# The 64-row chunk of a down projection on the two halves of the TensorE array, two token tiles at a time

## The chip, the cores and the metric

The kernel runs on one core of a Trainium2 chip. The metric is the device time of one execution in microseconds (us). A fast run has a granted TensorE clock (the clock that the chip lets the engine have) of 0.999 or 1.0 of full speed.

The profiles name the engines PE (TensorE, matmuls), PEld (TensorE loading weights), DVE (VectorE), ACT (ScalarE), POOL (GpSimd) and SP (SyncE, which issues most DMAs). PSUM is where matmuls add up their results; the kernel uses it in banks of 512 columns. In the down projection a matmul loads a tile's hidden values into the array as weights and streams columns of `w_down` past them; the 128 or 64 rows are the F columns that it sums over.

## The reference

An attention branch and a GEGLU feed-forward branch work on the same x (2048 tokens of width D = 640) and are mixed by a gate of each token. The change touches the last line of the feed-forward branch.

```python
g = sigmoid((x * gate_w).sum(-1, keepdims=True))
a = A_ref(x, wqkv, w_phi, wo)                     # linear attention with a softmax feature map, then @ wo
b = (gelu(x @ w_gate) * (x @ w_up)) @ w_down      # F = 1728 hidden columns
out = g * a + (1 - g) * b
```

F = 1728 is 13 chunks of 128 and one chunk of 64. Inputs and output are bf16.

## The kernel before

Each of the 16 token tiles (128 tokens) accumulates one result in PSUM: 14 chunks of F (hidden values times `w_down`) and then 5 chunks of the attention output times `wo`. Four tiles make a block. A block first computes its hidden values (gate and up products, stage `gateup`) and then runs `down` four times. The attention output of a tile (`num`) is computed in between; it uses PSUM banks 2 to 5 and about ten VectorE operations.

The last chunk of F has 64 real rows. The kernel before pads it with zeros to 128 rows and multiplies it like any other:

```python
# loads(): rows 0-63 of chunk 13 are zero, rows 64-127 real
sc.op("pool", lambda e: e.memset(self.wd_sb[0:64, 13, :], 0.0), writes=["wdz"])
sc.dma("sp", lambda e: e.dma_start(self.wd_sb[64:128, 13, :], self.wd[13 * P:self.F, :]), writes=["wd13"])
# ... (cut)
# gateup(), chunk 13: gate in rows 0-63 and up in rows 64-127 of one bank; the product goes to rows 64-127
sc.op("dve", lambda e: e.tensor_tensor(
    self.hT[64:128, c, :], self.ps[64:128, bk * 512:bk * 512 + 512], self.gl[64:128, slot, :], ALU.mult), ...)
# ... (cut)
def down(self, t, banks):                       # one token tile
    halves = ((banks[0], 0, 320), (banks[1], 320, 320))     # the last tile: 512 and 128 columns
    def step(c, bk, w0, w):
        if c < self.NFC:                        # NFC = 14 chunks of F, the last one half zeros
            sc.op("pe", lambda e: e.matmul(self.bank(bk, w), self.hT[:, c, tt * P:(tt + 1) * P],
                                           self.wd_sb[:, c, w0:w0 + w], start=(c == 0), stop=False), ...)
        else:                                   # 5 chunks of the attention output
            k = c - self.NFC
            sc.op("pe", lambda e: e.matmul(self.bank(bk, w), self.goT[:, gs, k, :],
                                           self.wo_sb[:, k, w0:w0 + w], start=False, stop=(k == self.KD - 1)), ...)
    # ... (cut) all steps, then ScalarE reads the two banks out and a DMA stores the tile
def ffn(self):
    pairs = [(6, 7), (0, 1)]                    # PSUM banks, in turn
    for b in range(self.NB):
        at = {2: 4 * b + 1, 6: 4 * b + 2, 10: 4 * b + 3}    # num(t) after these chunks; block 0 has its own list
        # ... (cut) gateup of 14 chunks, with num() as `at` says
        for t in range(4):
            self.down(4 * b + t, pairs[self.pn % 2])
            self.pn += 1
            if b == 0 and t == 0:
                self.num(3)
            if b < self.NB - 1 and t == 2:
                self.num(4 * b + 4)             # the next block's first tile
```

The softmax here doesn't subtract the row's maximum and nothing guards it: scores larger than these inputs give would overflow.

Of the kernel before, what the change touches and what calls it, by code (L numbers as in the profile page):

```python
# [3 lines left out]
P = 128  # L4
# [3 lines left out]
ALU = mybir.AluOpType  # L8
# [95 lines left out]
class _Kernel:  # L104
# [6 lines left out]
    NFC = 14  # L111
# [92 lines left out]
    def loads(self):  # L204
        sc, nc = self.sc, self.nc
# [22 lines left out]
        def xblock(b):  # L228
            sc.dma("sp", lambda e: e.dma_start_transpose(
                self.xT[:, :, b * self.BT:(b + 1) * self.BT], self.x[b * self.BT:(b + 1) * self.BT, :]),  # L230
                writes=[("xT", t) for t in range(b * 4, b * 4 + 4)])
# [2 lines left out]
        wload(self.wqT, 0, "wqT")  # L234
        xblock(2)
        xblock(3)
        sc.op("pool", lambda e: e.memset(self.wd_sb[0:64, 13, :], 0.0), writes=["wdz"])
        half = 7 * P
        g3 = self.wg.rearrange("(kt p) n -> p kt n", p=P)
        u3 = self.wu.rearrange("(kt p) n -> p kt n", p=P)  # L240
        for i, (a, b) in enumerate(((0, half), (half, 13 * P))):
            sc.dma("sp", lambda e, a=a, b=b: e.dma_start(self.wg_sb[:, :, a:b], g3[:, :, a:b]), writes=[("wg", i)])
            sc.dma("sp", lambda e, a=a, b=b: e.dma_start(self.wu_sb[:, :, a:b], u3[:, :, a:b]), writes=[("wu", i)])
            if i == 0:
# [1 line left out]
                sc.dma("sp", lambda e: e.dma_start(self.wgu_sb[:, :, 64:128], u3[:, :, 13 * P:self.F]), writes=["wgu1"])  # L246
        sc.dma("sp", lambda e: e.dma_start(self.wd_sb[:, 0:13, :],
                                           self.wd[0:13 * P, :].rearrange("(c p) n -> p c n", p=P)), writes=["wd"])
        sc.dma("sp", lambda e: e.dma_start(self.wd_sb[64:128, 13, :], self.wd[13 * P:self.F, :]), writes=["wd13"])
        sc.dma("sp", lambda e: e.dma_start(self.wo_sb[:, :, :], self.wo.rearrange("(kt p) n -> p kt n", p=P)),  # L250
               writes=["wo"])

# [7 lines left out]
        for i in range(KD):  # L260
            n = self.HHI[i] - self.HLO[i] + 1
# [9 lines left out]
        for i in range(KD):  # L271
            n = self.HHI[i] - self.HLO[i] + 1
# [332 lines left out]
    def gateup(self, b, c, banks):  # L605
        sc = self.sc
        xs = lambda kt: self.xT[:, kt, b * self.BT:(b + 1) * self.BT]
        xr = [("xT", t) for t in range(4 * b, 4 * b + 4)]
        oldw = self.oldw
        slot = self.gn % 3  # L610
        self.gn += 1
        if c < 13:
            i = 0 if c < 7 else 1
            for w, wk, bk in ((self.wg_sb, "wg", banks[0]), (self.wu_sb, "wu", banks[1])):
                for kt in range(self.KD):
                    sc.op("pe", lambda e, kt=kt, w=w, bk=bk: e.matmul(  # L616
                        self.bank(bk), w[:, kt, c * P:(c + 1) * P], xs(kt), start=(kt == 0), stop=(kt == self.KD - 1)),
                        reads=xr + [(wk, i)], writes=[("ps", bk)], signal=(kt == self.KD - 1))
            sc.op("act", lambda e: e.activation(self.gl[:, slot, :], self.bank(banks[0]), AF.Gelu_apprx_tanh),  # L619
                  reads=[("ps", banks[0])], writes=[("gl", slot)], guard=oldw)  # L620
            sc.op("dve", lambda e: e.tensor_tensor(self.hT[:, c, :], self.bank(banks[1]), self.gl[:, slot, :], ALU.mult),  # L621
                  reads=[("ps", banks[1]), ("gl", slot)], writes=[("hT", c)], guard=oldw)
        else:
            bk = banks[0]
            for kt in range(self.KD):
                sc.op("pe", lambda e, kt=kt: e.matmul(  # L626
                    self.bank(bk), self.wgu_sb[:, kt, :], xs(kt), start=(kt == 0), stop=(kt == self.KD - 1)),
                    reads=xr + ["wgu0", "wgu1"], writes=[("ps", bk)], signal=(kt == self.KD - 1))
            sc.op("act", lambda e: e.activation(self.gl[64:128, slot, :], self.ps[0:64, bk * 512:bk * 512 + 512],
                                                AF.Gelu_apprx_tanh),  # L630
                  reads=[("ps", bk)], writes=[("gl", slot)], guard=oldw)
            sc.op("dve", lambda e: e.tensor_tensor(
                self.hT[64:128, c, :], self.ps[64:128, bk * 512:bk * 512 + 512], self.gl[64:128, slot, :], ALU.mult),
                reads=[("ps", bk), ("gl", slot)], writes=[("hT", c)], guard=oldw)

    def num(self, t):
        sc = self.sc
# [43 lines left out]
        sc.dma("sp", lambda e: e.dma_start_transpose(self.goT[:, gs, :, :], self.Og[:, sl, :]),  # L681
               reads=[("Og", sl)], writes=[("goT", gs)], guard=old)

    def down(self, t, banks):
        sc = self.sc
        tt = t % 4
        gs = t % 6
        os_ = t % 3
        last = t == self.NT - 1
        halves = ((banks[0], 0, 512), (banks[1], 512, 128)) if last else ((banks[0], 0, 320), (banks[1], 320, 320))  # L690

        def step(c, bk, w0, w):
            if c < self.NFC:
                sc.op("pe", lambda e: e.matmul(  # L694
                    self.bank(bk, w), self.hT[:, c, tt * P:(tt + 1) * P], self.wd_sb[:, c, w0:w0 + w],
                    start=(c == 0), stop=False),
                    reads=[("hT", c)] + (["wd13", "wdz", "hTz"] if c == 13 else ["wd"]), writes=[("ps", bk)], signal=False)
            else:
                k = c - self.NFC
                sc.op("pe", lambda e: e.matmul(  # L700
                    self.bank(bk, w), self.goT[:, gs, k, :], self.wo_sb[:, k, w0:w0 + w],
                    start=False, stop=(k == self.KD - 1)),
                    reads=[("goT", gs), "wo"], writes=[("ps", bk)], signal=(k == self.KD - 1))

        def evac(bks, w0, n):
            src = self.pair(bks) if len(bks) == 2 else self.bank(bks[0], n)
            dst = self.outsb[:, os_, w0:w0 + n]
            if len(bks) == 2:
                dst = dst.rearrange("p (b c) -> p b c", c=320)
            sc.op("act", lambda e: e.activation(dst, src, AF.Copy, scale=self.Gm[:, t:t + 1]),  # L710
                  reads=[("ps", k) for k in bks] + ["Gm"], writes=[("outsb", os_, w)for w in ((0, 320) if n == 640 else (w0,))])
            rows = self.out[t * P:(t + 1) * P, :]
            if t < self.TB:
                rows = self.out[0:self.BT, :].rearrange("(p j) n -> p j n", j=self.TB)[:, t, :]
            sc.dma("sp", lambda e: e.dma_start(rows[:, w0:w0 + n], self.outsb[:, os_, w0:w0 + n]),
                   reads=[("outsb", os_, w) for w in ((0, 320) if n == 640 else (w0,))], writes=[("out", t, w0)])
        n = self.NFC + self.KD
        if last:
            for bk, w0, w in halves:
                for c in range(n):  # L720
                    step(c, bk, w0, w)
                evac((bk,), w0, w)
        else:
            for c in range(n):
                for bk, w0, w in halves:
                    step(c, bk, w0, w)
            evac(banks, 0, 640)

    NUMB = 2
    oldw = [(w, k) for w in ("wv", "wk2", "wq2") for k in range(5)] + ["wgate"]  # L730

    def ffn(self):
        self.gn = 0
        self.pn = 0
        self.sc.op("pool", lambda e: e.memset(self.hT[0:64, 13, :], 0.0), writes=["hTz"], guard=self.oldw)
        pairs = [(6, 7), (0, 1)]
        for b in range(self.NB):
            if b == 0:
                order = [0, 1, 13] + list(range(2, 13))
                at = {8: 0, 11: 1, 13: 2}  # L740
            else:
                order = list(range(14))
                at = {2: 4 * b + 1, 6: 4 * b + 2, 10: 4 * b + 3}
            for idx, c in enumerate(order):
                if b == 0 and c == 13:
                    self.gateup(b, c, (2,))
                else:
                    self.gateup(b, c, pairs[self.pn % 2])
                    self.pn += 1
                if b == 0:  # L750
                    if idx == 0:
                        self.gram(14)
                    if idx == 3:
                        self.gram(15)
                        self.kv_evac()
                        self.gates()
                    if idx == 6:
                        self.kv_mask()
                if idx in at:
                    self.num(at[idx])  # L760
            for t in range(4):
                self.down(4 * b + t, pairs[self.pn % 2])
                self.pn += 1
                if b == 0 and t == 0:
                    self.num(3)
                if b < self.NB - 1 and t == 2:
                    self.num(4 * b + 4)
def bass_gated_mix__linear_kernel_hedgehog__geglu_ffn__prompt_kernel(
    nc: bass.Bass,
    A_x: bass.AP,  # L770
    A_wqkv: bass.AP,
    A_w_phi: bass.AP,
    A_wo: bass.AP,
    B_x: bass.AP,
    B_w_gate: bass.AP,
    B_w_up: bass.AP,
    B_w_down: bass.AP,
    gate_w: bass.AP,
    out: bass.AP,
):  # L780
    _Kernel(nc, A_x, A_wqkv, A_w_phi, A_wo, B_x, B_w_gate, B_w_up, B_w_down, gate_w, out).run()
# [28 lines left out]
```

## Time and profile before

| | before |
|---|---|
| device time, median of 3 runs | 299.86 us (299.65 to 300.2) |
| span of the profiled run | 297.8 us |
| TensorE (PE) busy | 292.9 us, 98% |
| feed-forward stage in the chain (first gate matmul to the last matmul) | 84.72 to 295.08 us: 210.36 us |

The first lines are from the page of the kernel before: the share of busy time, the chain that ended last, and the largest group of the down projection (L694 is the matmul of the 14 chunks of F; L700, in the chain below, that of the 5 attention chunks).

```profile
span 297.8 us, 4821 instructions
PE 292.9 (98%) x1913; PEld 171.9 (58%) x1913; DVE 162.2 (54%) x318; ACT 104.3 (35%) x183; POOL 29.0 (10%) x58
PE 96%; DMA 1%; ACT 1%; issue 0%; SPq 0%; ACTq 0%
...
L694 PE MATMUL ps<-wd_sb,hT 128*128 128x320 bf16 (+2 forms) x448 | 63.6, 299 | 0.0
```

PE is the bottleneck, and in the feed-forward stage the chain never leaves it. The 299 ns of one matmul is not its cost, since matmuls overlap. The chain in order of time gives the cost; its columns are the start in us, the length in us, and what it was. These are the start of the feed-forward stage, block 1's change from gate/up (L616, L626) to its down projection, the `num` insert for the next block (L649), and the end:

```profile
84.72 1.24 PE ps L616 x5
...
168.25 1.08 PE ps L626 x5
169.33 3.80 PE ps L694 x28
173.14 1.36 PE ps L700 x10
...
184.82 0.69 PE ps L649 x12
185.51 3.80 PE ps L694 x28
189.31 1.36 PE ps L700 x10
190.67 6.47 PE ps L616 x30
...
294.79 0.29 PE ps L700 x5
```

A tile takes 28 matmuls in 3.80 us, 0.136 us each, and then 10 more at the same pace. Two of the 28 belong to the half-empty chunk. Over 16 tiles that chunk costs 30 x 0.136 us and, for the last tile, 0.216 + 0.056 us: 4.35 us, half of it spent on zeros.

A table of windows tells where VectorE works: here a gate/up stage and the down projection after it (the columns are the window, then busy time with the count of instructions for PE, weight loads, DVE, ACT, POOL, then clock, DMA share and GB/s).

```profile
138.13:169.33 31.20, 31.20 (x173) 15.29 (x172) 18.83 (x43) 8.56 (x14) 4.29 (x4) 1.00 0.10 22
169.33:190.67 21.34, 21.34 (x166) 15.54 (x164) 4.07 (x11) 2.97 (x4) 1.27 (x1) 1.00 0.15 32
```

DVE has 12 us free in the first and 17 us free in the second.

### The profile page before, as it was taken

Reading aid. Unit: us, or ns where it says so; the run is one execution under the profiler, and the core shown is the slowest. Engines: PE = TensorE matmul, PEld = TensorE weight load, DVE = VectorE, ACT = ScalarE, POOL = GpSimd, SP = SyncE. Lnnn points to the kernel's source line nnn. Section 1 sums busy time; section 2 is a strip of 40 time slices with the busy share of each in tenths; the row PEclk is TensorE's granted clock in tenths of the full one; section 3 lists DMA queues with packets and bytes.
Section 4 is the critical chain, followed back from the end, with each engine's and each line's share of the span. In section 5 each row is a group of like instructions: output and inputs, shape, how many; then the busy total and the mean of one; then the engine's idle time right before and its main releaser. Section 6 shows DMA issues by size and latency. Waiting matters only on the chain.

```text
span 297.8 us, 4821 instructions
## 1 busy us (share of the span) xinstructions
PE 292.9 (98%) x1913; PEld 171.9 (58%) x1913; DVE 162.2 (54%) x318; ACT 104.3 (35%) x183; POOL 29.0 (10%) x58
## 2 busy tenths in 40 slices
PE   7999999999999999999999999999999999999996
PEld 3576656555544556775555577655457765545763
DVE  1348999998875679514655700455580045567000
ACT  3367787576663221121222212122221212232111
POOL 7000000000000011201011100101110010111000
PEclk9999999999999999999999999999999999999999
DMA  7999990000002122112011200201101010110101
GB/s 219 211 209 335 355 350 18 0 0 2 0 2 53 35 20 28 47 44 66 3 22 22 20 27 24 60 6 25 22 9 37 22 46 23 22 24 0 44 24 44
DMA packets 38098, 18.77 MB, mean 63 GB/s; under 512 B 30203, under 2 KB 37820, under 8 KB 38076
## 3 DMA queue, kind: packets, MB, share of 16 engines
q1 hardware_dynamic: 37424, 18.44, 24.4%
q8 instruction: 15, 0.25, 0.3%
q10 hardware_dynamic: 652, 0.03, 0.1%
q14 instruction: 7, 0.06, 0.1%
HBM read 8.96 MB, written 2.62 MB: 39 GB/s over the span
## 4 chain that ended last, share of the span: by engine, by line
PE 96%; DMA 1%; ACT 1%; issue 0%; SPq 0%; ACTq 0%
PE ps L616 37%; PE ps L694 20%; PE ps L359 13%; PE ps L700 7%; PE ps L504 7%; PE ps L649 4%; PE ps L452 3%; PE ps L368 2%; PE ps L626 1%; DMA xtok<-in_A_x_dram 1%; PE ps L339 1%; ACT Eq L510 1%; ACT Ek L418 0%; PE ps L284 0%; PE ps L304 0%
## 5 line engine op out<-in xcount | busy, mean ns | idle before, releaser
L616 PE MATMUL ps<-xT,wu_sb 128*128 128x512 bf16 x260 | 64.6, 379 | 0.2 <-ACT Eq L510 0.2
L616 PE MATMUL ps<-xT,wg_sb 128*128 128x512 bf16 x260 | 64.6, 379 | 0.0
L694 PE MATMUL ps<-wd_sb,hT 128*128 128x320 bf16 (+2 forms) x448 | 63.6, 299 | 0.0
L621 DVE TENSOR_TENSOR hT<-ps,gl 128x512 bf16<-128x512 f32 x52 | 35.7, 688 | 44.5 <-PE ps L616 44.4
L619 ACT ACTIVATE gl<-ps 128x512 bf16<-128x512 f32 x52 | 31.1, 597 | 80.8 <-PE ps L616 78.6
L694 PEld LDWEIGHTS ps<-wd_sb,hT 128*128 128x128 bf16 x448 | 43.2, 98 | 17.8
L616 PEld LDWEIGHTS ps<-xT,wu_sb 128*128 128x128 bf16 x260 | 25.4, 98 | 31.1 <-issue 0.7
L359 PE MATMUL ps<-w,xT 128*128 128x512 bf16 (+3 forms) x240 | 40.9, 321 | 0.0
L616 PEld LDWEIGHTS ps<-xT,wg_sb 128*128 128x128 bf16 x260 | 25.0, 98 | 27.2
L710 ACT ACTIVATE outsb<-ps,Gm 128x640 bf16<-128x640 f32 (+2 forms) x17 | 13.0, 763 | 74.7 <-PE ps L700 74.7
L678 POOL TENSOR_TENSOR Og<-O,O 128x640 bf16<-128x640 bf16 x16 | 22.3, 1394 | 167.5 <-DVE O L676 167.5
L359 PEld LDWEIGHTS ps<-w,xT 128*128 128x128 bf16 x240 | 22.4, 97 | 18.2
L665 DVE RECIPROCAL RH<-ps 128x32 f32<-128x32 f32 x16 | 5.7, 358 | 40.7 <-PE ps L649 39.7
L429 DVE TENSOR_REDUCE Dk<-Ek 128x64 f32<-128x1280 bf16 x16 | 23.7, 1480 | 3.2 <-ACT gcol L421 3.2
L438 DVE TENSOR_TENSOR Ek<-Ek,Dk 128x640 bf16<-128x640 bf16 x32 | 25.0, 821 | 0.6
L504 PE MATMUL ps<-xT,wq 128*128 128x512 bf16 x100 | 24.7, 379 | 0.3 <-ACT Eq L510 0.3
L676 DVE TENSOR_TENSOR O<-ps,RH 128x640 bf16<-128x640 f32 x32 | 24.8, 816 | 0.0
L700 PE MATMUL ps<-wo_sb,goT 128*128 128x320 bf16 (+2 forms) x160 | 24.5, 299 | 0.0
L510 ACT ACTIVATE Eq<-ps 128x512 bf16<-128x512 f32 x40 | 21.7, 604 | 4.0 <-PE ps L504 4.0
L418 ACT ACTIVATE Ek<-ps 128x640 bf16<-128x640 f32 x32 | 20.7, 702 | 3.5 <-PE ps L359 3.5
L700 PEld LDWEIGHTS ps<-wo_sb,goT 128*128 128x128 bf16 x160 | 15.5, 98 | 6.3
L649 PEld LDWEIGHTS ps<-KV,Eq 128*128 128x128 bf16 x192 | 12.0, 98 | 3.1
(66 smaller groups left out, 154.2 us busy)
## 6 DMA issues: line engine op xcount, KB each, us to landing
out_dram<-outsb SPq DMA_DIRECT2D x15, 160.0 KB, 2.0
wd_sb<-in_B_w_down_dram SPq DMA_DIRECT2D x1, 2080.0 KB, 12.4
wg_sb<-in_B_w_gate_dram SPq DMA_DIRECT2D x1, 1120.0 KB, 5.7
wu_sb<-in_B_w_up_dram SPq DMA_DIRECT2D x1, 1120.0 KB, 9.6
wg_sb<-in_B_w_gate_dram SPq DMA_DIRECT2D x1, 960.0 KB, 9.9
wu_sb<-in_B_w_up_dram SPq DMA_DIRECT2D x1, 960.0 KB, 10.2
w<-in_A_wqkv_dram SPq DMA_DIRECT2D x5, 160.0 KB, 4.0
wo_sb<-in_A_wo_dram SPq DMA_DIRECT2D x1, 800.0 KB, 10.1
```

The source lines that it names most:

```text
L359: sc.op("pe", lambda e, kt=kt: e.matmul(self.bank(bank)[:, bcol:bcol + n], self.xT[:, kt, t * P:(t + 1) * P], self.w3[:, kt, c0:c0 + n], s ...
L429: sc.op("dve", lambda e: e.tensor_reduce(self.Dk[:, se, 0, :].rearrange("p (s h) -> p s h", h=H), self.Ek[:, se, :, :].rearrange("p s (h d ...
L438: sc.op("dve", lambda e, v=v, r=r: e.tensor_tensor(v, v, r, ALU.mult), reads=[("Rk", se)], writes=[("Ek", se, s)])
L504: sc.op("pe", lambda e, kt=kt: e.matmul(self.bank(bank), self.wq2[:, kt, i * P:(i + 1) * P], self.xT[:, kt, b * self.BT:(b + 1) * self.BT] ...
L510: sc.op("act", lambda e, s=s, scale=scale: e.activation(self.Eq[:, s, i, b * self.BT:(b + 1) * self.BT], self.bank(bank), AF.Exp, scale=sc ...
L616: sc.op("pe", lambda e, kt=kt, w=w, bk=bk: e.matmul(self.bank(bk), w[:, kt, c * P:(c + 1) * P], xs(kt), start=(kt == 0), stop=(kt == self. ...
L619: sc.op("act", lambda e: e.activation(self.gl[:, slot, :], self.bank(banks[0]), AF.Gelu_apprx_tanh), reads=[("ps", banks[0])], writes=[("g ...
L621: sc.op("dve", lambda e: e.tensor_tensor(self.hT[:, c, :], self.bank(banks[1]), self.gl[:, slot, :], ALU.mult), reads=[("ps", banks[1]), ( ...
L649: sc.op("pe", lambda e, s=s, i=i, n=n, o0=o0, k0=k0, bk=bk, r=r: e.matmul(self.bank(bk)[:, o0:o0 + n], self.Eq[:, s, i, t * P:(t + 1) * P] ...
L676: dve(lambda e, o=o, f=f, s=s: e.tensor_tensor(o, V[s][:, :, :, 0:DH], f, ALU.mult), rb + [key(6 + s)], [("O", s, sl)], guard=old)
L694: sc.op("pe", lambda e: e.matmul(self.bank(bk, w), self.hT[:, c, tt * P:(tt + 1) * P], self.wd_sb[:, c, w0:w0 + w], start=(c == 0), stop=F ...
L700: sc.op("pe", lambda e: e.matmul(self.bank(bk, w), self.goT[:, gs, k, :], self.wo_sb[:, k, w0:w0 + w], start=False, stop=(k == self.KD - 1 ...
```

## The change

The intent: let the half chunk of two token tiles run at once, one tile on array rows 0-63 and the other on rows 64-127, writing to different PSUM banks. For this the odd tiles keep their hidden values in rows 64-127, the even ones in rows 0-63, and `w_down`'s last 64 rows are loaded twice. All tiles of a block are done together (in block 0 two at a time), so that the array changes between full and half rows seldom. To have banks 2 to 5 free for this, `num` of a block's first tile moves from the previous down projection into the block's own gate/up stage. The diff, with cuts marked:

```diff
-        sc.op("pool", lambda e: e.memset(self.wd_sb[0:64, 13, :], 0.0), writes=["wdz"])
...
-        sc.dma("sp", lambda e: e.dma_start(self.wd_sb[64:128, 13, :], self.wd[13 * P:self.F, :]), writes=["wd13"])
+        for r in (0, 1):
+            sc.dma("sp", lambda e: e.dma_start(self.wd_sb[64 * r:64 * r + 64, 13, :], self.wd[13 * P:self.F, :]),
+                   writes=[("wd13", r)])
...
-            sc.op("dve", lambda e: e.tensor_tensor(
-                self.hT[64:128, c, :], self.ps[64:128, bk * 512:bk * 512 + 512], self.gl[64:128, slot, :], ALU.mult),
-                reads=[("ps", bk), ("gl", slot)], writes=[("hT", c)], guard=oldw)
+            for r in (0, 1):
+                odd = lambda v: v.rearrange("p (u r q) -> p u r q", r=2, q=P)[:, :, r, :]
+                sc.op("dve", lambda e: e.tensor_tensor(
+                    odd(self.hT[64 * r:64 * r + 64, c, :]), odd(self.ps[64:128, bk * 512:bk * 512 + 512]),
+                    odd(self.gl[64:128, slot, :]), ALU.mult),
+                    reads=[("ps", bk), ("gl", slot)], writes=[("hT", c, r)], guard=oldw)
...
+    def half(self, t, banks, h, first):
+        bk, w0, w = self.halves(t, banks)[h]
+        tt = t % 4
+        r = tt % 2
+        self.sc.op("pe", lambda e: e.matmul(
+            self.bank(bk, w), self.hT[64 * r:64 * r + 64, 13, tt * P:(tt + 1) * P],
+            self.wd_sb[64 * r:64 * r + 64, 13, w0:w0 + w], start=first, stop=False, skip_group_check=True),
+            reads=[("hT", 13, r), ("wd13", r)], writes=[("ps", bk)], signal=False)
+
+    def down_half(self, ts, banks):
+        for h in (0, 1):
+            for j, (t, bks) in enumerate(zip(ts, banks)):
+                self.half(t, bks, h, j > 0)
...
+        NFC = self.NFC - 1                      # in down(): 13 full chunks
...
             for c in range(n):
+                if c == NFC and extra:
+                    extra()
...
-        self.sc.op("pool", lambda e: e.memset(self.hT[0:64, 13, :], 0.0), writes=["hTz"], guard=self.oldw)
...
-                at = {2: 4 * b + 1, 6: 4 * b + 2, 10: 4 * b + 3}
+                at = {1: 4 * b, 4: 4 * b + 1, 7: 4 * b + 2, 10: 4 * b + 3}
...
-            for t in range(4):
-                self.down(4 * b + t, pairs[self.pn % 2])
-                self.pn += 1
-                if b == 0 and t == 0:
-                    self.num(3)
-                if b < self.NB - 1 and t == 2:
-                    self.num(4 * b + 4)
+            p = [pairs[(self.pn + k) % 2] for k in (0, 1)]
+            tiles = [4 * b + t for t in range(4)]
+            if b == 0:
+                for k in (0, 2):
+                    self.down(k, p[0], False, lambda: self.down_half((k, k + 1), p))
+                    if k == 0:
+                        self.num(3)
+                    self.down(k + 1, p[1], True)
+            else:
+                p += [(2, 3), (4, 5)]
+
+                def opening():
+                    self.down_half(tiles[0:2], p[0:2])
+                    for h in (0, 1):
+                        for t, bks in ((tiles[2], p[2]), (tiles[3], p[3])):
+                            self.half(t, bks, h, True)
+                for t, bks in zip(tiles, p):
+                    self.down(t, bks, t % 4 > 0, opening if t % 4 == 0 else None)
```

Below, an excursion is one run of 64-row matmuls between full ones: a switch to half rows and one back. Blocks 1 to 3 make one each, block 0 two: five in all.

More of the change, by code (lines that the diff above doesn't have):

```diff
@@ L682, in num, with halves, down @@
                reads=[("Og", sl)], writes=[("goT", gs)], guard=old)
-    def down(self, t, banks):
+    def halves(self, t, banks):
+        return ((banks[0], 0, 512), (banks[1], 512, 128)) if t == self.NT - 1 else ((banks[0], 0, 320), (banks[1], 320, 320))
+    def half(self, t, banks, h, first):
[10 more added lines that the diff above has]
+                self.half(t, bks, h, j > 0)
+    def down(self, t, banks, opened, extra=None):
         sc = self.sc
@@ L689, in down @@
         last = t == self.NT - 1
-        halves = ((banks[0], 0, 512), (banks[1], 512, 128)) if last else ((banks[0], 0, 320), (banks[1], 320, 320))
+        halves = self.halves(t, banks)
+        NFC = self.NFC - 1
         def step(c, bk, w0, w):
-            if c < self.NFC:
+            if c < NFC:
                 sc.op("pe", lambda e: e.matmul(
                     self.bank(bk, w), self.hT[:, c, tt * P:(tt + 1) * P], self.wd_sb[:, c, w0:w0 + w],
-                    start=(c == 0), stop=False),
-                    reads=[("hT", c)] + (["wd13", "wdz", "hTz"] if c == 13 else ["wd"]), writes=[("ps", bk)], signal=False)
+                    start=(c == 0 and not opened), stop=False, skip_group_check=True),
+                    reads=[("hT", c), "wd"], writes=[("ps", bk)], signal=False)
             else:
-                k = c - self.NFC
+                k = c - NFC
                 sc.op("pe", lambda e: e.matmul(
                     self.bank(bk, w), self.goT[:, gs, k, :], self.wo_sb[:, k, w0:w0 + w],
-                    start=False, stop=(k == self.KD - 1)),
+                    start=False, stop=(k == self.KD - 1), skip_group_check=True),
                     reads=[("goT", gs), "wo"], writes=[("ps", bk)], signal=(k == self.KD - 1))
@@ L716, in evac @@
                    reads=[("outsb", os_, w) for w in ((0, 320) if n == 640 else (w0,))], writes=[("out", t, w0)])
-        n = self.NFC + self.KD
+        n = NFC + self.KD
         if last:
```

## The prediction

> **What bounds the kernel now.** TensorE. The page gives PE 292.9 of 297.8 us busy, granted clock 1.0; the chain that ended last is 96% PE. In order of time, each token tile of the down projection shows there as 28 matmuls of L694 in 3.80 us and 10 of L700 in 1.36 us: 0.136 us per 128x320 matmul, though the profile prints 299 ns for one (they overlap; the pitch counts). PE waits for nobody from 84.7 to 295 us. By windows, DVE is busy 18.8 of 31 us while a block's gate/up matmuls run and 4.1 of 21.3 us in its down projection.
>
> **What the change removes.** The last F chunk, 64 real rows padded to 128, costs as much as a full one: 2 matmuls in each of 16 tiles, 30 x 0.136 us plus 0.216 + 0.056 us (512 and 128 columns of the last tile) = 4.35 us of the critical path. With two tiles streaming at once at best half of it, 2.17 us, goes. The two zero fills (POOL) lay on no chain: the first transposes wait for the x DMA (timeline).
>
> **What it adds on the path.** Changes of the array's tiling mode. The Trainium skill, "TensorEngine Tiling (Array Packing)", Key Properties, says that a mode switch drains the TensorEngine. This trace has one excursion, the 20-row and 1-row matmuls of L304/L312 at 9.5 us: the first starts about 0.10 us later than the stream of the last full one allows, the return costs about the same plus 0.01 (timeline, single instructions). Estimate: 0.105 us a switch. Block 0 has two excursions, blocks 1 to 3 one each: 10 switches, 1.05 us. "TensorE: Matmul & The Clock Gate", Part 3, gives a start offset of about 4 ns between tiles; the 1-column matmuls of L312 come 25 ns apart, so I allow 25 ns per excursion. No pair on different rows is in this trace: that they overlap is untested here.
>
> Excursion of four tiles: before 8 x 0.136 = 1.09 us; after 4 x 0.136 + 0.21 + 0.025 = 0.78 us; gain 0.31. Of two tiles: 0.54 against 0.51; gain 0.04. Sum: 3 x 0.31 + 2 x 0.04 = 1.0 us.
>
> **What it moves.** The attention output of a block's first tile moves from the previous down projection into the gate/up stage (every third chunk instead of every fourth). Its PE time (12 matmuls, 0.69 us) stays. DVE does one such tile in about 4.0 us; the next product then ends about 5.5 us after the chunk, and its bank is wanted at 6.1 us, as before; three chunks plus the insert take 7.2 us, DVE needs about 6.1. So no new PE wait, but 0.6 us of margin. The hT product of chunk 13 becomes two 64x256 pieces, about 0.4 us each instead of 0.69: ready about 1.9 us after the last gate/up matmul, wanted after 3.5 us. Banks 2-5 are drained well before they are reopened.
>
> **Predicted time:** 298.9 us, 8 in 10 between 297.9 and 300.2. Faster by over 2%: 0.01; within 2%: 0.98; slower by over 2%: 0.01.
>
> **What would show it.** In the chain, full chunks keep 0.136 us a matmul; the half matmuls take about 0.78 us in blocks 1 to 3 and 0.51 us per excursion of block 0, 64-row matmuls starting in twos a few to 25 ns apart; about 0.1 us lost on each side; PE idle still near zero; DVE's time up by about 4 us in the gate/up windows of blocks 1 to 3, down by it in the down windows before them.
>
> **What would make it wrong.** Halves that do not overlap (weight loads or writes serialising): then +1 us instead of -1. A switch dearer than 0.2 us each way. A PE wait at the moved attention outputs or at the opening matmuls.

## The result, and the profile after

| | before | after |
|---|---|---|
| device time, median of 6 runs each | 299.75 us | 298.82 us |
| ratio, 95% interval | | 0.9969 [0.9956, 0.9983] |
| feed-forward stage in the chain | 210.36 us | 294.61 - 85.36 = 209.25 us |

Every ratio in this text is the mean time of one kernel's fast runs over that of the kernel before's fast runs of the same rounds, so it is not quite the ratio of the medians. The interval excludes no change: the changed kernel is 0.3% faster.

The same lines of the page of the changed kernel. L716 is now the matmul of the 13 full chunks, L722 that of the attention chunks, L695 the half matmul.

```profile
span 297.3 us, 4821 instructions
PE 292.5 (98%) x1913; PEld 170.3 (57%) x1913; DVE 162.6 (55%) x322; ACT 104.3 (35%) x183; POOL 28.0 (9%) x56
PE 93%; SPq 2%; DMA 2%; ACT 1%; issue 0%; ACTq 0%
...
L716 PE MATMUL ps<-wd_sb,hT 128*128 128x320 bf16 (+2 forms) x416 | 59.3, 299 | 0.0
```

The share of PE did not move: 98% before and after, so it does not show the gain. The Trainium skill warns in "Perfetto Trace Analysis", Identifying the Most-Contended Engine, that matmul busy time is not a good measure of how close a kernel is to its limit, because matmuls are pipelined. The chain in order of time does say something, because it gives the pace. Block 0 (its `num` inserts are L653), block 1, and the ends of the stage:

```profile
85.36 1.24 PE ps L617 x5
...
120.27 0.38 PE ps L695 x4
120.65 1.47 PE ps L722 x10
...
168.78 1.08 PE ps L627 x5
169.86 3.53 PE ps L716 x26
173.39 0.65 PE ps L695 x8
174.04 1.47 PE ps L722 x10
175.50 3.53 PE ps L716 x26
179.03 1.36 PE ps L722 x10
...
294.32 0.29 PE ps L722 x5
```

A tile's full chunks keep their pace (26 in 3.53 us). The eight half matmuls of block 1 take 0.65 us instead of the 8 x 0.136 = 1.09 us that they took padded, and the ten L722 matmuls after them take 1.47 instead of 1.36 us: the chain puts the switch back there. Together 0.65 + 0.11 = 0.76 us an excursion. In block 0, 0.38 + 0.11 = 0.49 us for four half matmuls, instead of 0.54.

The timeline around that excursion has the weight loads too (start, length, engine, group, and in brackets how long the engine was idle before):

```profile
173.09 0.30 PE L716 MATMUL ps<-wd_sb,hT 128*128 128x320 bf16 x1
173.32 0.39 PEld L695 LDWEIGHTS ps<-wd_sb,hT 64*128 64x128 bf16 x8 [0.26 <-issue]
173.32 0.72 PE L695 MATMUL ps<-wd_sb,hT 64*128 64x320 bf16 x8
173.97 0.39 PEld L722 LDWEIGHTS ps<-wo_sb,goT 128*128 128x128 bf16 x4 [0.26 <-issue]
173.97 0.58 PE L722 MATMUL ps<-wo_sb,goT 128*128 128x320 bf16 x3
```

At both ends of the excursion no weights are loaded ahead: the first weight load and the first matmul of the new kind start together. The single records of the same stretch, read from the trace to the nanosecond (this is not a view of the profile), in us from the start of the last full matmul:

```text
0.000            matmul, 128 rows (the last full one; the next would start at 0.136)
0.228 0.231      two weight loads, rows 0-63 and rows 64-127
0.232 0.235      two matmuls, 64 rows each            0.096 late
0.378 0.381      the next two                         0.146 after the first, 0.010 over the pace
0.514 0.517      the next two                         0.136
0.650 0.653      the last two                         0.136
0.877            weight load, 128 rows
0.881            matmul, 128 rows                     0.231 after the last two: 0.095 late
1.028            the next                             0.147: 0.011 over the pace
```

So pairs do run at once, here 3 ns apart and 2 to 4 ns in the others of equal width, which agrees with the 4 ns of the page that the prediction names; four pairs stream in the time of four matmuls. And an excursion loses 0.096 + 0.010 + 0.095 + 0.011 = 0.212 us to its two switches, where the prediction had 0.210.

A rival is that the lateness comes not from the change of rows but from a semaphore wait: in this stretch the first weight load at each end carries one. The single records settle it (the n-th weight load belongs to the n-th matmul). In e3 (below), 12 of the 16 first loads on the way in and 8 of the 16 on the way back carry none, and their matmuls are as late (0.095 us or more); in the kernel before, 147 loads of the stage carry one between full-row matmuls, and none of their matmuls comes over 0.001 us late.

VectorE, in the windows of block 1:

```profile
137.96:169.86 31.90, 31.90 (x185) 16.00 (x184) 22.12 (x53) 8.56 (x14) 5.58 (x4) 1.00 0.10 22
169.86:190.17 20.31, 20.31 (x153) 14.29 (x152) 0.85 (x2) 2.98 (x4) 0.00 (x0) 1.00 0.17 34
```

The moved attention output is the 3.3 us that DVE gained in the first window (18.83 to 22.12) and lost, but for the slightly longer product of chunk 13, in the second (4.07 to 0.85). PE is busy through both windows in both kernels, and the views of waits show none for PE between 90 and 294 us in either.

One difference lies outside the stage: the changed kernel's profiled run entered it 0.64 us later (85.36 against 84.72). The chain has it waiting for the transposed load of the key weights in the start-up (the DMA and SPq shares of the page's chain). That is looked at in the experiments.

### The profile page after: what moved, and what is told of

It is laid out like the page before. It is cut to its first block, busy times and chain, and to the rows that moved or that the text cites. A ratio compares the mean times of both kernels' runs of the same rounds, so it can differ in the third digit from the quotient of the medians.

```text
span 297.3 us, 4821 instructions
## 1 busy us (share of the span) xinstructions
PE 292.5 (98%) x1913; PEld 170.3 (57%) x1913; DVE 162.6 (55%) x322; ACT 104.3 (35%) x183; POOL 28.0 (9%) x56
## 4 chain that ended last, share of the span: by engine, by line
PE 93%; SPq 2%; DMA 2%; ACT 1%; issue 0%; ACTq 0%
PE ps L617 37%; PE ps L716 19%; PE ps L360 12%; PE ps L722 7%; PE ps L505 7%; PE ps L653 4%; PE ps L453 3%; DMA wkT<-in_A_wqkv_dram 2%; PE ps L627 1%; SPq L229 1%; PE ps L340 1%; PE ps L695 1%; SPq L216 1%; ACT Eq L511 1%; ACT Ek L419 0%
## 5 line engine op out<-in xcount | busy, mean ns | idle before, releaser
L716 PE MATMUL ps<-wd_sb,hT 128*128 128x320 bf16 (+2 forms) x416 | 59.3, 299 | 0.0
L716 PEld LDWEIGHTS ps<-wd_sb,hT 128*128 128x128 bf16 x416 | 40.2, 98 | 16.8
L722 PE MATMUL ps<-wo_sb,goT 128*128 128x320 bf16 (+2 forms) x160 | 24.6, 299 | 0.0
L722 PEld LDWEIGHTS ps<-wo_sb,goT 128*128 128x128 bf16 x160 | 15.1, 98 | 7.2 <-issue 1.3
L653 PEld LDWEIGHTS ps<-KV,Eq 128*128 128x128 bf16 x192 | 12.0, 98 | 3.6
L653 PE MATMUL ps<-KV,Eq 128*128 128x154 bf16 x192 | 13.7, 221 | 0.0
```

Of the source, the lines that this page charges most:

```text
L653: sc.op("pe", lambda e, s=s, i=i, n=n, o0=o0, k0=k0, bk=bk, r=r: e.matmul(self.bank(bk)[:, o0:o0 + n], self.Eq[:, s, i, t * P:(t + 1) * P] ...
```

## The experiments

Two batches, each on one chip, with 5 rounds against the kernel before. The stage is again read from the chain: its first gate matmul to its last matmul. Differences of under 0.3 us are better read from the stage, which repeats to 0.01 us (see e7 and e8), than from the times.

| run | excursions | median us | ratio to before, 95% interval | stage us | stage against before |
|---|---|---|---|---|---|
| before | 0 | 299.75 | 1 | 210.36 | 0 |
| after | 5 | 298.82 | 0.9969 [0.9956, 0.9983] | 209.25 | -1.11 |
| e1_same_rows | 5, nothing at once | 301.06 | 1.0034 [1.002, 1.0049] | 211.42 | +1.06 |
| e2_two_excursions | 8 | 299.31 | 0.9977 [0.9964, 0.9989] | 209.89 | -0.47 |
| e3_four_excursions | 16 | 300.94 | 1.0039 [1.002, 1.0058] | 211.67 | +1.31 |
| e5_block0_once | 4 | 298.64 | 0.9951 [0.9937, 0.9965] | 209.04 | -1.32 |
| e4_moved_only | 0 | 300.0 | 0.9994 [0.998, 1.0008] | 210.37 | +0.01 |
| e6_no_half_chunk (wrong result) | 0 | 295.26 | 0.9843 [0.9828, 0.9858] | 206.02 | -4.34 |
| e7_after_again | 5 | 298.95 | 0.9962 [0.995, 0.9975] | 209.25 | -1.11 |
| e8_block0_once_again | 4 | 298.6 | 0.995 [0.9937, 0.9962] | 209.04 | -1.32 |

The kernel before had a median of 300.04 us in the first batch (e1, e2, e3, e5) and 299.97 us in the second.

### e1_same_rows: half rows, but never two tiles at once

All four tiles keep their half chunk in rows 0-63. The 64-row matmuls and the excursions stay; only the overlap goes.

```diff
-        r = tt % 2
+        r = 0
...
-            for r in (0, 1):
-                odd = lambda v: v.rearrange("p (u r q) -> p u r q", r=2, q=P)[:, :, r, :]
+            for r in (0,):
+                odd = lambda v: v
...
-        for r in (0, 1):
+        for r in (0,):                          # the load of the last 64 rows of w_down
```

> The half chunk stays in 64-row matmuls and in the same five excursions, but all four tiles use the upper half of the array, so no two can stream at once. Theory (the gain is the overlap of two tiles, less ten mode switches): nothing of the 4.35 us is saved and the switches stay, so about 5 x 0.21 = 1.05 us slower than the kernel before, 300.8 us, and 2.0 us slower than the changed kernel; an excursion of four tiles 1.29 us in the chain instead of 0.65 plus the late start after it. Rival (the gain comes from the moved attention outputs, the missing zero fills or the shorter contraction itself): about 298.9 us, as the changed kernel.

Measured: 301.06 us, ratio 1.0034, stage +1.06 us. The chain of block 1 in this run:

```profile
170.17 3.53 PE ps L716 x26
173.70 1.19 PE ps L695 x8
174.89 1.46 PE ps L722 x10
```

The excursion takes 1.19 us against 0.65, and as before another 0.1 us falls to the matmuls after it. All of the gain is therefore the overlap, and the price of the switches shows alone: 1.06 us over five excursions. The shorter contraction by itself saves nothing: 64 rows take as long as 128, since (1.19 - 0.65) us are four matmuls of 0.136 us. The rival falls.

### e2_two_excursions: blocks 1 to 3 as block 0

```diff
-                for t, bks in zip(tiles, p):
-                    self.down(t, bks, t % 4 > 0, opening if t % 4 == 0 else None)
+                for k in (0, 2):
+                    self.down(tiles[k], p[k], False, lambda: self.down_half(tiles[k:k + 2], p[k:k + 2]))
+                    self.down(tiles[k + 1], p[k + 1], True)
```

> Blocks 1 to 3 do their half chunk as block 0 does, in two excursions of two tiles each: 8 excursions instead of 5, the same pairs. Theory: 3 more excursions at 0.21 us, so 0.63 us slower than the changed kernel, 299.5 us, and still 0.3 us faster than before. Rival (a switch is hidden or nearly free, or the count of excursions does not matter): 298.9 us.

Measured: 299.31 us, stage 209.89 us, which is 0.64 us over the changed kernel for three more excursions: 0.213 us each. The rival (a free switch) falls.

### e3_four_excursions: every pair alone

The two pairs of two tiles are set apart, with four full matmuls between them.

```diff
-    def down_half(self, ts, banks):
-        for h in (0, 1):
-            for j, (t, bks) in enumerate(zip(ts, banks)):
-                self.half(t, bks, h, j > 0)
+    def down_half(self, ts, banks, hh):
+        for j, (t, bks) in enumerate(zip(ts, banks)):
+            self.half(t, bks, hh, j > 0)
...
-                if c == NFC and extra:
-                    extra()
+                if c - NFC in (0, 2) and extra:
+                    extra((c - NFC) // 2)
...                                             # and tiles two by two in all blocks, as in e2
```

> Every pair of half matmuls stands alone between full ones: 16 excursions instead of 5, the same 32 overlapping half matmuls. Theory: 11 more excursions at 0.21 us, so 2.3 us slower than the changed kernel, 301.2 us, which is 1.4 us slower than the kernel before although every pair still overlaps. Rival (a short excursion costs less because there is less to drain): under 300 us.

Measured: 300.94 us, ratio 1.0039, stage +1.31 us. Block 1 shows where it goes; each excursion of one pair is 0.24 us, and the matmuls after it are 0.11 us longer than 4 or 6 x 0.136:

```profile
169.74 3.53 PE ps L715 x26
173.27 0.24 PE ps L695 x2
173.51 0.65 PE ps L721 x4
174.16 0.24 PE ps L695 x2
174.40 0.92 PE ps L721 x6
```

Against the changed kernel the stage is 2.42 us longer for 11 more excursions (expected 2.3). Of this 0.08 us is not a switch: the last tile is split into 512 and 128 columns, and its 512-column matmul, alone with one of 320 columns, holds up the return by 0.216 - 0.136 us. In the single records 15 of the 16 excursions lose 0.209 to 0.213 us and that one 0.08 us more; 11 at 0.213 make 2.34 us, and 2.34 + 0.08 = 2.42. So the price is of the excursion and does not shrink with its length, and with the very same 32 overlapping matmuls the row tiling is a loss. The rival falls.

### e4_moved_only: the kernel before with `num` moved

```diff
-                at = {2: 4 * b + 1, 6: 4 * b + 2, 10: 4 * b + 3}
+                at = {1: 4 * b, 4: 4 * b + 1, 7: 4 * b + 2, 10: 4 * b + 3}
...
-                if b < self.NB - 1 and t == 2:
-                    self.num(4 * b + 4)
```

> The kernel before with only the attention outputs moved as the change moves them (each block's first one from the previous down projection into the gate/up stage, every third chunk). Theory: VectorE keeps up, no TensorE wait appears, the FFN stage of the chain stays 210.4 us long: 299.8 us, within 0.3 us of the kernel before. Rival (the move itself brings part of the gain, or costs something that the row tiling pays back): off by 0.5 us or more either way, with a wait or a shorter stage in the chain.

Measured: 300.0 us beside 299.97, ratio 0.9994 with an interval on both sides of 1, stage 210.37 us. The move is free, and brings nothing. The rival falls.

### e6_no_half_chunk: the floor

The half matmuls are left out, and with them all switches of the stage. The result is wrong (relative error 0.17).

```diff
-                    self.down(k, p[0], False, lambda: self.down_half((k, k + 1), p))
+                    self.down(k, p[0], False)
...                                             # likewise in blocks 1 to 3; every down() starts its own sum
```

> Wrong result on purpose: the changed kernel without its 32 half matmuls and so without any switch in the FFN; everything else as in it. Theory: the padded half chunk cost the kernel before 4.35 us and costs the changed one 3.2 us (2.17 us of streaming and 10 switches), so this floor is about 4.35 us faster than before, 295.4 us, FFN stage 206.0 us. Rival (the half chunk was partly hidden, or the switches cost less than thought and something else was lost): a floor 1 us or more away from that.

Measured: 295.26 us, stage 206.02 us, from the first and the last piece of the stage in its chain:

```profile
84.58 1.24 PE ps L617 x5
...
290.31 0.29 PE ps L722 x5
```

The half chunk therefore cost the kernel before 210.36 - 206.02 = 4.34 us (4.35 was worked out from the pace), and it costs the changed kernel 209.25 - 206.02 = 3.23 us. Nothing of it was hidden. The rival falls.

### e5_block0_once: one excursion in block 0 too

The restriction in block 0 is that `num(3)` holds banks 2 to 5 during the down projection. This version lets tiles 0 and 1 run without their half chunk, with `num(3)` between them as before, and then closes tiles 0 and 1 and opens tiles 2 and 3 in one excursion.

```diff
-                for k in (0, 2):
-                    self.down(k, p[0], False, lambda: self.down_half((k, k + 1), p))
-                    if k == 0:
-                        self.num(3)
-                    self.down(k + 1, p[1], True)
+                p += [(2, 3), (4, 5)]
+                self.down(0, p[0], False, part="open")      # 13 + 5 chunks, no stop, no read-out
+                self.num(3)
+                self.down(1, p[1], False, part="open")
+                for k in (0, 2):
+                    for h in (0, 1):
+                        for t in (k, k + 1):
+                            self.half(t, p[t], h, k == 2, k == 0)   # starts tiles 2, 3; stops tiles 0, 1
+                self.down(0, p[0], True, part="evac")
+                self.down(1, p[1], True, part="evac")
+                self.down(2, p[2], True)
+                self.down(3, p[3], True)
```

> A version that may beat both: block 0 also does its four tiles in one excursion, after tiles 0 and 1 (closed by it) and before tiles 2 and 3 (opened by it), so 4 excursions instead of 5. Theory: one excursion less, 0.21 us faster than the changed kernel, 298.65 us, about 1.3 us faster than before, if banks 2 to 5 are read out in time (the attention output of tile 3 ends on VectorE about 4.2 us after its matmuls, the excursion comes 4.9 us after them). Rival: a new wait at the excursion eats it, 298.9 us or more.

Measured: 298.64 us, ratio 0.9951 [0.9937, 0.9965], correct. Its chain in block 0:

```profile
122.17 3.53 PE ps L716 x26
125.70 1.36 PE ps L722 x10
127.06 0.65 PE ps L695 x8
127.71 3.64 PE ps L716 x26
```

The excursion follows tile 1 without a wait (0.65 us for eight half matmuls, as in blocks 1 to 3), so banks 2 to 5 were read out in time. The stage is 209.04 us, 0.21 us shorter than the changed kernel's: one excursion. This version beats the kernel before, and in the stage the changed kernel too; e7 and e8 compare those two side by side.

### e7_after_again and e8_block0_once_again: both once more, on one chip

No edit to the changed kernel and to e5.

> The changed kernel unaltered, beside the one-excursion version on the same chip. Expected 1.0 us faster than before; the FFN stage again 209.25 us; its start (85.36 us in the first profile, 84.72 us in the kernel before) differs by some tenths from profile to profile if the late start was the start-up transfers' scatter; if the change caused it, it is again at 85.3 us or later.

> The version with one excursion in block 0 once more, beside the changed kernel on the same chip: 0.2 us faster than it, FFN stage again 209.04 us.

Measured: 298.95 us (0.9962) and 298.6 us (0.995); the stages are 209.25 and 209.04 us again. The intervals of the two ratios to the kernel before overlap (from 0.995 to 0.9962), but both hold the scatter of that kernel too. Directly, all five runs of e8 (298.44 to 298.72 us) are below all five of e7 (298.75 to 299.18 us), and the stages agree: the version with four excursions is faster, by 0.21 us in the stage.

The stage's start in the ten profiles answers the other question. It was at 84.72 us (before), 85.33 us (e4, whose start-up is that of the kernel before), and 85.36, 85.22, 85.13, 85.03, 84.81, 85.21, 84.94 and 84.58 us in the runs with the changed start-up (after, e7, e1, e2, e3, e5, e8, e6). Both kinds are found at both ends of 0.8 us. The 0.64 us of the first comparison is the scatter of the start-up, and no cost of the change was found in it. Single times of one kernel in one batch spread by 0.3 us (e8) to 1.9 us (e3); the stage repeats to 0.01 us (after and e7, e5 and e8).

## Why the prediction was right

It forecast 298.9 us and a gain of 1.0 us; measured were 298.82 us and, in the stage, 1.11 us. The stated range, 297.9 to 300.2 us, also holds the 299.75 us of the kernel before, so that the time landed in it proves little; the stage and the chain carry the proof. Point by point:

- What bounds the kernel: right. PE has no wait in the stage before or after, and the cost of the half chunk, 4.35 us from the pace, is 4.34 us by e6.
- The overlap: right, though the trace before had no example of it. Pairs start 2 to 4 ns apart, and without the overlap (e1) the whole gain is gone and the switches remain.
- The price of a switch: right. The new excursions show 0.106 us a switch (half of 0.212) for the predicted 0.105. That they agree so closely is partly luck. The one excursion of the kernel before, at 9.5 us, has other rows (20 and 1) and shows 0.096 + 0.010 us on the way in; on the way back the next matmul starts 0.091 us after a 1-column one and loses another 0.010. How much of the 0.091 is the switch depends on the pace of a 1-column matmul: 0.066 if it is the 0.025 that the others beside it show. So that excursion costs 0.18 to 0.21 us, and the prediction took the upper end. Five variants with 4 to 16 excursions fit it: the stage less the floor of e6 less the 2.17 us of overlapped streaming leaves 0.85, 1.06, 1.70 and 3.48 us for 4, 5, 8 and 16 excursions (e5, after, e2, e3; e3's 3.48 holds the 0.08 us of its last tile), and 1.06 us for e1's five when its full 4.34 us are taken off: 0.212 to 0.213 us each.
- The sum: the allowance of 25 ns an excursion for the start of pairs was not needed. An excursion of four tiles is 0.755 us where 0.78 was predicted, one of two tiles 0.484 us where 0.51 was. That explains the 0.11 us between the predicted 1.0 and the measured 1.11 us: 5 x 0.025 = 0.125 us saved, and about 0.01 us more for the switches.
- The move of `num`: right; no new wait, and e4 shows that it has no effect on time. The shift of VectorE's work was predicted at about 4 us a block and was 3.3 us; the 4.07 us of the window before also hold 0.69 us of the product of chunk 13, which stays. The pieces of the hT product were expected at about 0.4 us; the trace has 426 to 428 ns.
- The zero fills: expected to be off every chain. No run isolates them; the stage's sum closes to 0.01 us without them, and the start-up shows no trend between runs with and without them.

What stays open: why a switch takes 0.1 us. The trace shows that no weights of the new kind are loaded ahead (the first weight load starts 4 ns before its matmul, where it otherwise starts about 0.13 us before), and that the cost is the same after a 160-column matmul (at 9.5 us) as after a 320-column one. Whether the array has to empty or only the loading ahead is lost, these runs do not tell apart. They also do not tell how close VectorE may come to holding PE up. The prediction put its margin at 0.6 us; by the records, in blocks 1 to 3 the shortest time from the end of a product of VectorE to the matmul that needs its bank again is 0.88 us, in both kernels.

## What to carry to other kernels

Row tiling of the half-empty chunk halved its streaming time here (4.34 to 2.17 us), but each excursion into it cost a fixed 0.21 us, so count excursions before counting matmuls: of the 2.17 us that the overlap could save, 1.06 us went to five of them, and with sixteen it was a loss. Collect the half chunks of as many tiles as PSUM can hold open at once, and put them at the point in the order where their banks are already free, even if that closes some tiles' sums and opens others' (e5). Price such a change from the pace in the chain and from the switches that the kernel already makes; the busy share of PE was 98% in all ten profiles.

## What the Trainium skill lacked or had wrong

- "TensorEngine Tiling (Array Packing)", Key Properties, says that a mode switch drains the TensorEngine, but gives no cost. Here it was 0.106 us a switch and 0.212 us an excursion, with two or four pairs in it, and 0.213 us with one; the break-even lies between one pair of 320 columns (0.136 us saved) and two (0.27 us).
- "TensorE: Matmul & The Clock Gate", Back-to-back issue gap, gives 131 ns a matmul of 512 columns and 81 ns of 128 columns as the sustained spacing with weight loads in between. Here, with a weight load for each matmul, 30 of 512 columns took 6.47 us in the chain (216 ns each) and 14 of 128 columns 0.78 us (56 ns each), the figures that the page has in that section for single matmuls in isolation, and in Part 1 for back-to-back ones.
- The same page, Part 3, says under "What overlaps and what doesn't" that a weight load overlaps running matmuls only when it goes to other rows of the array (its paragraph on the mechanism also allows a background weight buffer). Here weight loads to the same rows began 1 to 2 ns after the previous matmul's start and cost nothing, both with full rows (0.136 us a matmul of 320 columns) and in e1 with the same 64 rows (0.136 us too).
- Its start offset of about 4 ns between row tiles was confirmed: 2 to 4 ns for two tiles of 64 rows with matmuls of equal width.
